# Windowed attention feeding a SwiGLU block on one core: a shorter lead and a new order of attention, with six instead of four chunks of q and k turned on the matmul array

## The chip, the cores and the metric

One core of one Trainium2 chip. The time is the device time of one execution in microseconds (us), fast executions only. A ratio is the mean time of one kernel's fast runs over that of the other's in the same rounds, so it is not quite the ratio of the medians quoted beside it. Two kernels are compared within one group of runs on the same chip, because the kernel before gave medians of 371.2 to 372.2 us from group to group. PE is the matmul engine, DVE the vector engine, ACT the scalar engine, POOL the general engine, SP the queue that issues all DMAs here, in order.

## The reference

Causal attention with a window of 64 keys, then a SwiGLU feed-forward block on its output:

```python
# q, k, v: (8 batches, 8 heads, 576 tokens, 64), float32
scores = q @ k^T / 8;  masked to 0 <= i - j < 64;  softmax;  times v
x = attention output as (4608 tokens, 512)
g = x @ w_gate                       # 512 x 1536
out = (g * sigmoid(g) * (x @ w_val)) @ w_out
```

## The kernel before

The 4608 tokens go through as 18 *chunks* of 256 (loads and turns of q and k), 36 *groups* of 128 (scores, products with v, turn of x, projection) and 9 *tiles* of 512 (twelve feed-forward steps each). Every engine executes its instructions in the order in which the program states them. So the text fixes how far attention runs ahead of the feed-forward (its *lead*).

q and k must be turned so that the head dimension lies on partitions. There are two ways. On the array, eight PE transposes go into PSUM and one copy brings them out:

```python
def turn2(n, nm, eng):                 # rows hold token pairs (load: 512 B runs)
    x_b = words.pop((nm, n))
    tp = ps_a.tile([P, 4, 2, P], BF16, name="tp", tag="a")
    for c in range(2):
        for p in range(4):
            nc.tensor.transpose(tp[:, p, c], x_b[:, c, P * p:P * p + P], identb[:])
    ...
    copy(eng, y, tp[:].rearrange("r p c x -> r p x c"))
```

By DMA, two transposes stand on the same queue as the loads:

```python
def turn1(n, nm):                      # rows hold single tokens (load1: 256 B runs)
    x_b = words.pop((nm, n))
    for i in range(2):
        ...
        sp.dma_start_transpose(out=ring[:, :, o:o + P], in_=x_b[:, i])
```

A feed-forward step uses two PSUM banks each for g and v. A step's banks are free again when DVE has done the `finish` of it, which is stated one step later:

```python
def step(t, m, c0=0, n=512):
    st = gv(t, m, c0, n)               # PE: 4 matmuls into g_ps, 4 into v_ps; ACT: tanh of g
    if pend: finish(pend)              # DVE: sg = (th + 1) * g;  hT = sg * v
    pend = st
```

`scores(g)` puts on PE the scores, on ACT their exponential E, on DVE the multiplication of E by the mask. `products(g)` is E times v on PE, with a normalisation on DVE into `x_b`. `turn_x(g)` is four transposes on PE and a copy on ACT into `xT`, the input of the feed-forward. All three share three PSUM banks (`ps_a`). F, A and B are full steps and half steps (first or second half of a tile). After a hand-ordered start the loop does one group per pass:

```python
for w in range(8, NG):
    t, s = divmod(w, 4); n, odd = w // 2, w % 2
    step(t, 3 * s)
    scores(w + 6);  turn_x(w + 4)
    ...                                 # casts of k (odd w) or q (even w) on POOL
    step(t, 3 * s + 1)
    products(w + 5, (0,));  cast_v(w + 6, pool)
    step(t, 3 * s + 2)
    products(w + 5, (1,))
    ...                                 # turn1 of k (odd, chunk n + 5) or q (even, chunk n + 4)
    project(t - 1, s)
    ...                                 # load1 and load_v of later chunks
```

(The bounds on w are cut.) Chunks 0 to 3 are turned on the array, 4 to 17 by DMA.

The softmax here doesn't subtract the row's maximum and nothing guards it: scores larger than these inputs give would overflow.

## Time and profile before

| | before |
|---|---|
| time, median of 2 | 371.24 us |
| span of the profiled execution | 370.2 us |
| PE busy | 93% |
| mean granted clock | 0.989 |
| PE idle before the scores of chunk 6 and of chunk 7 | 2.56 and 2.00 us |
| first loop step starts | 104.35 us |
| first pass of the loop | 12.66 us |
| later passes (21, from the projection in pass 8 to that in pass 29), each | 9.12 us |

A timeline row gives start, duration, engine, line, operation, output and inputs, and a count. A bracket gives the idle time of the engine before it and what ended it. A table by stages gives the stretch and its length, then busy time and number of instructions for PE, weight loads, DVE, ACT and POOL, then granted clock, DMA share and GB/s. The lines themselves stand in the prediction. First DVE, then PE, in pass 11 (w = 11 in the loop):

```profile
137.93 1.52 DVE L168 TENSOR_TENSOR E<-E,mask 128x512 bf16<-128x512 bf16 x2 [2.98 <-ACT E L167]
139.37 0.68 DVE L248 SCALAR_TENSOR_TENSOR sg<-th,g_ps 128x512 f32<-128x512 f32 x1
```
```profile
140.09 1.02 PE L237 MATMUL g_ps<-xT,wg 128*128 128x512 bf16 x3 [0.53 <-DVE sg L248]
```

DVE does the masks first and only then the `sg` that gives back a g bank. PE asks for that bank one step (1.73 us) after the scores, so it starts when `sg` ends, at 140.05. Slow masks: two of them took 1.52 us here, while POOL was casting v (137.14 to 139.17).

### The profile page before, as it was taken

How to read it: one execution, taken by the hardware profiler on the slowest of the kernel's cores; microseconds unless marked ns; L12 is line 12 of the kernel's file. 1: busy time of each engine (PE TensorE's matmuls, PEld its weight loads, DVE VectorE, ACT ScalarE, POOL GpSimd, SP SyncE). 2: the span in 40 equal slices, each digit the busy share in tenths (PEclk: the TensorE clock that was granted, in tenths of full speed). 3: DMA queues.
4: the chain of work that ended last, by engine and by line, in shares of the span. 5: the costliest groups of instructions: out<-in, count | busy, mean ns of one | idle time of the engine just before them, and what ended most of it. 6: DMA issues, size and time to landing. Idle time of an engine off the chain costs nothing.

```text
span 370.2 us, 7165 instructions
## 1 busy us (share of the span) xinstructions
PE 345.2 (93%) x2750; PEld 181.5 (49%) x2797; DVE 231.1 (62%) x503; ACT 154.0 (42%) x276; POOL 113.5 (31%) x159
## 2 busy tenths in 40 slices
PE   8787998989779999999999999999999999999995
PEld 3456556546334444444444545444444445444442
DVE  5577798697245666666666666666666666644520
ACT  3554755444243443444344444444444443323311
POOL 2554585463314350605060606060605120000000
PEclk9999999999899999999999999999999999999999
DMA  8999999899889965857688869675744300001112
GB/s 204 322 252 266 290 313 241 150 159 188 176 186 186 197 149 119 175 124 158 132 172 120 177 123 149 147 168 126 143 96 104 87 28 30 28 30 41 44 58 85
DMA packets 147841, 54.99 MB, mean 149 GB/s; under 512 B 127328, under 2 KB 141664, under 8 KB 147808
## 3 DMA queue, kind: packets, MB, share of 16 engines
q1 hardware_dynamic: 147808, 54.54, 66.6%
q8 instruction: 22, 0.36, 0.5%
q14 instruction: 11, 0.09, 0.1%
HBM read 37.75 MB, written 9.44 MB: 127 GB/s over the span
## 4 chain that ended last, share of the span: by engine, by line
PE 74%; DVE 6%; DMA 6%; SPq 5%; ACT 5%; issue 2%; POOL 2%; ACTq 0%; POOLq 0%
PE o_ps L254 24%; PE g_ps L237 21%; PE v_ps L237 19%; DMA q_f<-in_q_dram 4%; SPq L93 4%; DVE E L168 3%; PE s_ps L161 3%; PE w_ps L266 2%; ACT E L167 2%; PE xtp L205 2%; PE ao_ps L183 2%; PE ao_ps L187 2%; DMA qT<-q_fb 1%; DVE sg L248 1%; SPq L123 1%
## 5 line engine op out<-in xcount | busy, mean ns | idle before, releaser
L237 PE MATMUL g_ps<-xT,wg 128*128 128x512 bf16 (+1 forms) x457 | 111.9, 358 | 6.9 <-DVE sg L248 4.8
L237 PE MATMUL v_ps<-xT,wv 128*128 128x512 bf16 (+1 forms) x472 | 112.3, 360 | 0.9 <-ACT wv L103 0.5
L254 PE MATMUL o_ps<-wo,hT 128*128 128x512 bf16 x419 | 98.4, 384 | 0.7
L242 ACT ACTIVATE th<-g_ps 128x512 f32<-128x512 f32 (+1 forms) x120 | 67.3, 561 | 71.0 <-PE g_ps L237 66.9
L248 DVE SCALAR_TENSOR_TENSOR sg<-th,g_ps 128x512 f32<-128x512 f32 (+1 forms) x120 | 75.1, 626 | 20.9 <-ACT th L242 20.9
L168 DVE TENSOR_TENSOR E<-E,mask 128x512 bf16<-128x512 bf16 x72 | 36.9, 526 | 74.8 <-ACT E L167 73.4
L249 DVE TENSOR_TENSOR hT<-sg,v_ps 128x512 bf16<-128x512 f32 (+1 forms) x120 | 76.1, 634 | 8.4
L237 PEld LDWEIGHTS <-wv 128*128 128x128 bf16 x480 | 47.0, 98 | 48.3 <-issue 1.4
L237 PEld LDWEIGHTS <-wg 128*128 128x128 bf16 x480 | 44.8, 98 | 41.7 <-issue 7.0
L254 PEld LDWEIGHTS <-hT 128*128 128x128 bf16 x432 | 40.8, 99 | 46.1 <-issue 2.2
L105 POOL CAST q_fb<-q_f 128x1024 bf16<-128x1024 f32 x17 | 17.9, 1053 | 114.6 <-DMA q_f<-in_q_dram 112.4
L167 ACT ACTIVATE E<-s_ps 128x512 bf16<-128x512 f32 x72 | 39.1, 596 | 20.1 <-PE s_ps L161 20.1
L105 POOL CAST ve<-v_f 64x512 bf16<-64x512 f32 x71 | 44.3, 624 | 4.4
L192 DVE TENSOR_TENSOR x_b<-ao_ps,r 128x256 bf16<-128x256 f32 x72 | 30.5, 424 | 2.5
L105 POOL CAST vo<-v_f 128x512 bf16<-128x512 f32 x36 | 22.3, 621 | 25.8 <-DMA v_f<-in_v_dram 14.2
L105 POOL CAST k_fb<-k_f 128x1024 bf16<-128x1024 f32 x17 | 18.1, 1063 | 38.1 <-DMA k_f<-in_k_dram 32.6
L183 PE MATMUL ao_ps<-ve,E 128*128 128x65 bf16 x288 | 26.6, 194 | 2.2 <-DVE x_b L192 1.2
L183 PEld LDWEIGHTS <-E 128*128 128x128 bf16 x288 | 22.0, 98 | 9.6 <-DVE E L168 1.5
L187 PE MATMUL ao_ps<-vo,E 128*128 128x65 bf16 x288 | 26.6, 194 | 0.0
L206 ACT COPY xT<-xtp 128x512 bf16<-128x512 bf16 x36 | 21.2, 590 | 12.1 <-PE xtp L205 12.1
L187 PEld LDWEIGHTS <-E 128*128 128x128 bf16 x288 | 20.1, 98 | 6.5 <-issue 0.3
L161 PE MATMUL s_ps<-qT,kT 64*128 64x64 bf16 x576 | 14.9, 191 | 7.3 <-DMA qT<-q_fb 4.6
(73 smaller groups left out, 136.3 us busy)
## 6 DMA issues: line engine op xcount, KB each, us to landing
v_f<-in_v_dram SPq DMA_DIRECT2D x32, 256.0 KB, 4.8
k_f<-in_k_dram SPq DMA_DIRECT2D x25, 256.0 KB, 3.9
q_f<-in_q_dram SPq DMA_DIRECT2D x25, 256.0 KB, 4.2
w_f<-in_moe_w_gate_dram SPq DMA_DIRECT2D x6, 512.0 KB, 7.6
w_f<-in_moe_w_val_dram SPq DMA_DIRECT2D x6, 512.0 KB, 6.5
wo_f<-in_moe_w_out_dram SPq DMA_DIRECT2D x6, 512.0 KB, 6.5
k_f<-in_k_dram SPq DMA_DIRECT2D x3, 512.0 KB, 6.9
q_f<-in_q_dram SPq DMA_DIRECT2D x3, 512.0 KB, 8.1
```

The lines of the kernel that those rows point to most:

```text
L105: eng.tensor_copy(y, x)
L161: nc.tensor.matmul(ps[a][:, p, 1 - b], kT[g // 2 % KR][y, p, o:o + P], qT[g // 2 % QR][y, p, o:o + 64], tile_position=(64 * a, 0),)
L167: act.activation(e, ps[a][:], AF.Exp, scale=0.125)
L168: dve.tensor_mul(e, e, mk[:].unsqueeze(1).to_broadcast([P, 4, 2, 64]))
L183: nc.tensor.matmul(o_ps[:, i, :], E[:, e + P:e + 2 * P], ve[g % VR][:, y, :], start=True, stop=False,)
L187: nc.tensor.matmul(o_ps[:, i, :], E[:, e:e + P], vo[g % VR][:, y, :], start=False, stop=True,)
L192: dve.tensor_mul(x_b[:, 256 * h:256 * h + 256].rearrange("r (y d) -> r y d", y=4), o_ps[:, :, 0:D], r[:].unsqueeze(2).to_broadcast([P, 4, D]),
L237: nc.tensor.matmul(ps[:, 0:n], w[:, c, P * m:P * m + P], xT[t][:, c, c0:c0 + n], start=(c == 0), stop=(c == 3),)
L242: act.activation(th[:, 0:n], g_ps[:, 0:n], AF.Tanh, scale=0.5)
L248: dve.scalar_tensor_tensor(sg[:, 0:n], th[:, 0:n], 1.0, g_ps[:, 0:n], ALU.add, ALU.mult)
L249: dve.tensor_mul(hT[t][:, m, c0:c0 + n], sg[:, 0:n], v_ps[:, 0:n])
L254: nc.tensor.matmul(o_ps[:], hT[t][:, c, P * s:P * s + P], wo[:, c, :], start=(c == 0), stop=(c == 11),)
```

## The change

Intent: let attention run only four to five groups ahead instead of five to six, so that loads, casts and turns are wanted later; take chunks 4 and 5 off the DMA transposes; in the loop, do the products after the first step and the scores after the second.

```diff
+    load(4, k, "k_f")                  # was load1
+    load(4, q, "q_f")
...
-    turn1(4, "k_f")
-    turn1(4, "q_f")
     ...                                # and load(5, ...) follows at once
+    turn2(4, "k_f", dve)               # between F(1, 7) and F(1, 8)
+    turn2(4, "q_f", act)               # between F(1, 8) and F(1, 9)
...
+    turn2(5, "k_f", dve)               # before project(0, 1)
+    turn2(5, "q_f", act)               # between B(1, 3) and B(1, 4)
...
+    scores(12)
+    load1(8, k, "k_f")
     project(0, 3)
+    turn_x(11)

     for w in range(8, NG):
         step(t, 3 * s)
-        scores(w + 6);  turn_x(w + 4)
+        products(w + 4)
+        ...casts for chunks one earlier than before
         step(t, 3 * s + 1)
-        products(w + 5, (0,))
+        scores(w + 5);  turn_x(w + 4)
         step(t, 3 * s + 2)
-        products(w + 5, (1,))
         ...                            # turns and loads for chunks one earlier
         project(t - 1, s)
```

(Cut to its core; bounds left out. The order of the second tile's steps is shuffled too: the first half runs to A(1, 6), the second to B(1, 6), every projection of tile 0 stands between attention parts, and the casts move with them.)

More of the change, by code (lines that the diff above doesn't have):

```diff
@@ L413 @@
     turn_x(5)
-    load1(4, k, "k_f")
-    load1(4, q, "q_f")
+    load(4, k, "k_f")
+    load(4, q, "q_f")
     load_v(4)
+    cast_k(3, "k_f", pool)
     F(0, 10)
-    cast_k(3, "k_f", pool)
     cast_k(3, "q_f", pool)
+    keys_before(3)
+    turn2(3, "k_f", dve)
+    F(0, 11)
+    turn2(3, "q_f", act)
     cast_v(6, pool)
     cast_v(7, pool)
-    F(0, 11)
-    keys_before(3)
-    turn2(3, "k_f", dve)
     A(1, 0)
-    turn2(3, "q_f", act)
+    for s in range(2):
+        casts_o(s, pool)
     A(1, 1)
-    for s in range(3):
-        casts_o(s, pool)
-    A(1, 2)
-    scores(6)
-    A(1, 3)
-    scores(7)
-    products(6)
-    for s in range(3, 6):
-        casts_o(s, pool)
-    A(1, 4)
-    turn_x(6)
-    products(7)
+    scores(6)
+    A(1, 2)
+    scores(7)
+    A(1, 3)
+    products(6)
+    A(1, 4)
+    products(7)
+    turn_x(6)
+    for s in range(2, 4):
+        casts_o(s, pool)
     A(1, 5)
@@ L443 @@
     cast_k(4, "q_f", pool)
-    turn1(4, "k_f")
-    turn1(4, "q_f")
-    keys_before(4)
-    load1(5, k, "k_f")
-    load1(5, q, "q_f")
-    load_v(5)
-    B(1, 0)
-    F(1, 6)
+    load(5, k, "k_f")
+    load(5, q, "q_f")
+    load_v(5)
+    A(1, 6)
+    B(1, 0)
+    for s in range(4, 6):
+        casts_o(s, pool)
+    B(1, 1)
+    F(1, 7)
+    keys_before(4)
+    turn2(4, "k_f", dve)
     cast_v(8, pool)
     cast_v(9, pool)
-    F(1, 7)
+    F(1, 8)
+    turn2(4, "q_f", act)
+    F(1, 9)
     scores(8)
-    F(1, 8)
+    project(0, 0)
+    B(1, 2)
+    scores(9)
     products(8)
-    F(1, 9)
-    turn_x(8)
-    scores(9)
     cast_k(5, "k_f", pool)
     cast_k(5, "q_f", pool)
-    turn1(5, "k_f")
-    turn1(5, "q_f")
-    keys_before(5)
     load1(6, k, "k_f")
@@ L469 @@
     F(1, 10)
+    turn_x(8)
     products(9)
@@ L474 @@
     turn_x(9)
-    scores(10)
-    project(0, 0)
-    B(1, 1)
-    products(10)
-    B(1, 2)
+    keys_before(5)
+    turn2(5, "k_f", dve)
+    project(0, 1)
+    B(1, 3)
+    turn2(5, "q_f", act)
     cast_k(6, "k_f", pool)
+    turn1(6, "k_f")
+    keys_before(6)
     cast_k(6, "q_f", pool)
-    turn1(6, "k_f")
     turn1(6, "q_f")
-    keys_before(6)
     load1(7, k, "k_f")
@@ L487 @@
     load_v(7)
+    B(1, 4)
+    scores(10)
+    project(0, 2)
+    products(10)
+    B(1, 5)
+    scores(11)
     turn_x(10)
-    scores(11)
-    project(0, 1)
-    B(1, 3)
+    B(1, 6)
     products(11)
     cast_v(12, pool)
-    B(1, 4)
-    turn_x(11)
-    scores(12)
-    project(0, 2)
-    B(1, 5)
-    products(12)
-    cast_v(13, pool)
     cast_k(7, "k_f", pool)
@@ L503 @@
     keys_before(7)
-    cast_k(7, "q_f", pool)
-    turn1(7, "q_f")
+    scores(12)
     load1(8, k, "k_f")
-    load1(8, q, "q_f")
-    scores(13)
     project(0, 3)
-    cast_k(8, "k_f", pool)
-    turn1(8, "k_f")
-    keys_before(8)
-    load1(9, k, "k_f")
+    turn_x(11)
     for w in range(8, NG):
@@ L519 @@
         step(t, 3 * s)
-        if w + 6 < NG:
-            scores(w + 6)
+        if w + 4 < NG:
+            products(w + 4)
+        if odd and n + 4 < NB:
+            cast_k(n + 4, "k_f", pool)
+        if not odd and n + 3 < NB:
+            cast_k(n + 3, "q_f", pool)
+        if w + 5 < NG:
+            cast_v(w + 5, pool)
+        step(t, 3 * s + 1)
+        if w + 5 < NG:
+            scores(w + 5)
         if w + 4 < NG:
             turn_x(w + 4)
-        if odd and n + 5 < NB:
-            cast_k(n + 5, "k_f", pool)
-        if not odd and n + 4 < NB:
-            cast_k(n + 4, "q_f", pool)
-        step(t, 3 * s + 1)
-        if w + 5 < NG:
-            products(w + 5, (0,))
-        if w + 6 < NG:
-            cast_v(w + 6, pool)
-        step(t, 3 * s + 2)
-        if w + 5 < NG:
-            products(w + 5, (1,))
-        if odd and n + 5 < NB:
-            turn1(n + 5, "k_f")
-            keys_before(n + 5)
-        if not odd and n + 4 < NB:
-            turn1(n + 4, "q_f")
+        step(t, 3 * s + 2)
+        if odd and n + 4 < NB:
+            turn1(n + 4, "k_f")
+            keys_before(n + 4)
+        if not odd and n + 3 < NB:
+            turn1(n + 3, "q_f")
         project(t - 1, s)
         if odd and n + 5 < NB:
-            load1(n + 5, q, "q_f")
+            load1(n + 5, k, "k_f")
         if odd and n + 4 < NB:
             load_v(n + 4)
-        if not odd and n + 6 < NB:
-            load1(n + 6, k, "k_f")
+        if not odd and n + 4 < NB:
+            load1(n + 4, q, "q_f")
     flush()
```

## The prediction

> **What bounds the kernel now.** I read the page first, then the chain of waits, the timeline of the matmul engine (PE) around its largest gaps, the table by stages, and the DMA queue's own timeline. The kernel has one core, so there is no slow die to set aside.
>
> ```profile
> PE 345.2 (93%) x2750; PEld 181.5 (49%) x2797; DVE 231.1 (62%) x503; ACT 154.0 (42%) x276; POOL 113.5 (31%) x159
> PEclk9999999999899999999999999999999999999999
> ```
>
> PE is the bound. Its one dip in granted clock is the eleventh of the forty slices, 93 to 102 us. The table by stages (columns: stretch, length, busy time and instructions of PE, weight loads, DVE, ACT, POOL, then clock, DMA share, GB/s) says the same:
>
> ```profile
> 51.50:68.00 16.50, 14.05 (x159) 9.91 (x160) 13.97 (x35) 8.08 (x16) 12.31 (x15) 1.00 0.97 248
> 68.00:91.70 23.70, 22.38 (x236) 13.38 (x237) 18.80 (x42) 11.05 (x22) 9.27 (x12) 1.00 0.99 176
> 91.70:104.35 12.65, 9.57 (x83) 4.92 (x83) 5.31 (x14) 3.67 (x8) 5.32 (x8) 0.87 0.88 193
> 104.35:117.00 12.65, 10.60 (x72) 5.00 (x72) 6.88 (x15) 3.95 (x7) 2.93 (x4) 0.87 0.87 166
> 117.00:306.00 189.00, 185.11 (x1474) 93.37 (x1501) 121.89 (x257) 80.99 (x147) 57.43 (x82) 1.00 0.67 135
> ```
>
> From 117 us on PE has little left to give. The loss is in the two stretches from 91.7 to 117 us. PE's timeline names the event in each:
>
> ```profile
> 91.59 0.62 PE L205 MATMUL xtp<-identb,x_b 128*128 128x128 bf16 x4
> 94.77 0.41 PE L161 MATMUL s_ps<-qT,kT 64*128 64x64 bf16 x16 [2.56 <-DMA qT<-q_fb]
> 95.11 4.45 PE L254 MATMUL o_ps<-wo,hT 128*128 128x512 bf16 x11
> ...
> 101.75 2.76 PE L254 MATMUL o_ps<-wo,hT 128*128 128x512 bf16 x11
> ...
> 108.24 0.41 PE L161 MATMUL s_ps<-qT,kT 64*128 64x64 bf16 x16 [2.00 <-DMA qT<-q_fb]
> ...
> 110.12 1.91 PE L237 MATMUL v_ps<-xT,wv 128*128 128x512 bf16 x4
> ```
>
> The scores of chunk 6, then of chunk 7, wait for q to come back from a DMA transpose. After each wait the same matmuls run slowly: 4.45 instead of 2.76 us, and 1.91 instead of the 1.03 seen elsewhere. The chain shows that this is the end of a long series, not two late transfers:
>
> ```profile
> 57.87 5.67 DMA q_f<-in_q_dram
> 63.64 1.04 POOL q_fb L105
> 66.62 2.09 SPq L123
> 70.73 5.00 DMA q_f<-in_q_dram
> 75.88 1.24 POOL q_fb L105
> 79.23 1.44 SPq L123
> ...
> 85.00 4.92 DMA q_f<-in_q_dram
> 90.07 1.04 POOL q_fb L105
> 92.18 2.46 DMA qT<-q_fb
> ```
>
> Load, cast, transpose (L123, on the same in-order queue as the loads), next load: about 13 us per chunk of 256 tokens. A transpose on the queue holds the next loads back until its own cast is done.
>
> **What the Trainium skill says.** (1) "TensorE: Matmul & The Clock Gate", section "What's actually happening": PE falls to half clock after an idle window of about 3.4 us and needs as much busy time to return. The trace agrees in kind: the granted clock was 0.60 from 95.1 to 99.4 and 0.57 from 108.8 to 112.0 us, though the gaps were only about 2.8 and 2.3 us. (2) The same page, "Part 4: PE-mode transpose": a 128x128 transpose of about 275 ns in one kernel, whose result lies in PSUM and must be copied out. Here one takes 219 ns, eight in a row hold PE 0.45 us, and the copies take 1.22 us (DVE, k) and 1.01 us (ACT, q). (3) "SBUF — State Buffer", "Who interferes with whom": a DVE instruction with two SBUF inputs and a GpSimd instruction that reads SBUF exclude each other. The mask multiply (L168) has two such inputs; its shortest was 409 ns and its longest 1250 ns, which agrees. (4) "DMA: Bandwidth & Descriptors", "Why small descriptors are slow (HBM only)": a 256 B descriptor pays a fixed cost per packet. No row of this trace isolates that; I give it no number.
>
> **The change part by part.** Engine order is program order here, so I step the three busy engines by hand with durations from the trace: a full feed-forward step 1.73 us of PE (8 matmuls of 0.216) and 1.38 of DVE (half steps 0.87 and 0.85), scores 0.34, products 0.48 (DVE 1.10), a turn of x 0.33, a projection 2.59.
>
> *Removed:* the DMA transposes of chunks 4 and 5, 8 of 56. On the queue they took 2.72 + 3.36 and 2.87 + 3.10 us, 12.0 in all. Chunk 5's loads now follow chunk 4's at once and no longer wait behind casts, and both use 512 B runs.
>
> *Added:* 32 transposes on PE, 4 x 0.45 = 1.8 us, on the path; two DVE copies (2.4 us) and two ACT copies (2.0 us), which only partly fit beside PE.
>
> *51.5 to 68 us.* DVE is busy 85% here. Stepping it: half steps of group 1 arrive at 0.87, DVE retires them at 0.85 but must also do two score masks and two products (about 4 us), so DVE sets the pace before and after. The extra half step after the turn of x hides one ACT copy. I get the step F(1,7) starting at 67.5 instead of 68.0: gain 0.5.
>
> *67.5 us to the start of the loop.* PE work: five full steps 8.65, five halves 4.35, five scores 1.7, four products 1.9, four turns of x 1.3, four projections 10.4, four chunk turns 1.8: 30.1 us. I find stalls at the second bank of products(8) (0.35), the q copy before scores(10) (0.4), the mask before products(11) (0.5), the free bank in scores(12) (0.6), and small ones: about 2.1. Loop start 99.7 instead of 104.35.
>
> *Does chunk 6 still make PE wait?* Its loads follow the output of project(0,0) at about 77.7, are issued by 85, and the last q lands near 85 to 86 (5 to 6 us after issue, as before). The queue then reaches the transposes after the output of project(0,1), at 87.7, two pairs of 2.7 us: q is turned by about 93. PE asks at about 95.9: 2.8 us to spare. Chunk 7: turned near 106, asked for at 112.6.
>
> *The loop.* Work of one pass is 3 x 1.73 + 0.34 + 0.48 + 0.33 + 2.59 = 8.93 us. From the project at 114.58 to the one at 306.03, 21 passes take 9.12 each: 3.3 us over the shortest (8.96). DVE's masks sit between the first step and the finish that frees its bank, so a mask slowed by a POOL cast stalls PE (0.53 us at 140.1). After the change the products come after the first step and the masks only after the second, followed by a step and a projection (4.3 us) before that bank is asked for. Collisions stop hurting; I credit 2.5 us.
>
> *Sum.* Start of the loop: 104.35 - 99.7 = 4.65 earlier, less one scores and one products (0.82) not yet done: 3.8. First pass: before it took 104.35 to 117.01 = 12.66, of which 3.7 over a normal 8.96: saved. Later passes 2.5. Total 10.0. I take off 0.8 for waits that a hand stepping misses: 9.2. The timed 371.24 becomes 362.0 us (2.5% less).
>
> **The rivals.** *A: the waits only move.* With a lead of four to five groups instead of five to six, the transposes reach scores later. Steady state: q's transposes run in an even pass after 0.7 + 1.2 + 3 us of loads, landing 8.4 us into it; scores want them 4.0 us into the next, 4.5 us to spare. Landings ranged up to 5.0 us in the trace against the 2.5 median, so mostly safe. If chunk 6 is late all the same, 1 to 2 us of wait and as much of slow clock return: 364 to 366. If the loop waits in each second pass by 0.5 us, 7 us go: 369. *B: DVE becomes the bound before 100 us.* It is 85 and 79% busy in the two stretches ahead of 91.7 us and gets 2.4 us more. If neither copy hides, the loop starts at 102: about 364. *C: only the waits were lost, and the loop was at its floor.* Then 2.5 us of credit fall away: 364.5. *D: more comes.* No stall at all before the loop and the floor in every pass: 359.
>
> **Range and chances.** 362.0 us, 8 in 10 within 358.5 to 367.0. The limit for faster by 2% is 363.8; B or C in full would miss it narrowly, in part they would not. Faster 0.68, within 2% 0.30, slower 0.02: slower needs waits in most passes, against 4.5 us of slack.
>
> **What would show it.** Right: no granted clock below 0.95 between 90 and 120 us; no PE wait on a qT transfer; the loop's first step near 99 to 100 us; 48 DMA transposes, chunk turns on PE up by 32; project-to-project time near 8.97 with longer masks but no PE wait on the feed-forward gate multiply after 110 us. Wrong: scores waiting on DMA in the loop (A), PE waiting on DVE between 55 and 95 us by more than 4 us (B), passes still at 9.1 (C).

## The result

362.06 us (two runs, 361.73 and 362.39) against 371.24: ratio 0.9753, 95% interval 0.9711 to 0.9795. Two later groups, of six runs of the changed kernel and eleven of the kernel before each, gave 361.74 against 371.28 (0.9752) and 361.52 against 372.06 (0.9717).

| | before | after |
|---|---|---|
| time, median | 371.24 us | 362.06 us |
| profiled span | 370.2 us | 359.8 us |
| F(1,7) starts | 68.00 us | 67.20 us |
| first loop step starts | 104.35 us | 100.71 us |
| first pass | 12.66 us | 8.92 us |
| later passes, each | 9.12 us | 8.92 us |
| PE idle before the scores of chunk 6 / 7 for q | 2.56 / 2.00 us | none / none |
| mean granted clock | 0.989 | 0.998 |

The page of the profile after, busy times and the clock row:

```profile
PE 340.8 (95%) x2790; PEld 181.2 (50%) x2837; DVE 233.1 (65%) x507; ACT 155.9 (43%) x279; POOL 112.9 (31%) x159
PEclk9999999999999999999999999999999999999999
```

The dip in the clock row is gone. The table by stages, cut at the same events as in the prediction (turn of chunk 3 to F(1,7), to the loop, first pass, passes to the projection in pass 29):

```profile
51.50:67.20 15.70, 14.47 (x170) 10.74 (x169) 13.82 (x35) 8.11 (x18) 8.40 (x10) 1.00 1.13 262
67.20:100.70 33.50, 30.56 (x316) 18.55 (x320) 23.46 (x55) 16.50 (x31) 14.64 (x21) 1.00 0.79 146
100.70:109.63 8.93, 8.86 (x71) 4.42 (x72) 5.82 (x12) 3.26 (x6) 4.94 (x7) 1.00 1.25 213
109.63:294.60 184.97, 182.82 (x1474) 92.03 (x1501) 124.45 (x259) 80.95 (x147) 58.23 (x83) 1.00 0.74 142
```

The start of the loop is 3.64 us earlier (0.80 of it already at F(1,7)). The first pass is 3.74 us shorter. The 21 passes that follow took 191.45 us from projection to projection before (114.42 to 305.87) and take 187.39 now (107.04 to 294.43): 4.06 us. The remainder is 1.04 us longer, of which one scores and one products (0.82 us), moved into the loop's end, explain most. 3.64 + 3.74 + 4.06 - 1.04 = 10.4 us, the difference of the two spans. The timed medians differ by only 9.2: the profiled execution of the kernel before was itself 0.9 us slower than its median.

The queue of the changed kernel, where chunk 6 is turned, and PE where it is asked for, up to the first loop step; the last line is PE where chunk 7 is asked for:

```profile
87.33 2.61 SPq L123 DMA_TRANSPOSE kT<-k_fb  x2
90.03 2.53 SPq L123 DMA_TRANSPOSE qT<-q_fb  x2
```
```profile
95.58 0.20 PE L161 MATMUL s_ps<-qT,kT 64*128 64x64 bf16 x1
96.45 0.40 PE L161 MATMUL s_ps<-qT,kT 64*128 64x64 bf16 x15 [0.68 <-DVE x_b L192]
97.02 2.54 PE L254 MATMUL o_ps<-wo,hT 128*128 128x512 bf16 x11 [0.16 <-issue]
...
100.71 1.02 PE L237 MATMUL g_ps<-xT,wg 128*128 128x512 bf16 x4 [0.94 <-ACT xT L206]
...
113.67 0.41 PE L161 MATMUL s_ps<-qT,kT 64*128 64x64 bf16 x16
```

The first of the two q transposes of chunk 6, which holds the tokens that these scores use, has landed at 92.4 (2.4 us after its issue), three us before PE asks. q of chunk 7 is through the queue at 107.6. What PE waits for now is local: a bank of `ps_a` (0.68), and the copy of the turn of x(11), which stands directly ahead of the step that needs it (0.94).

### The profile page after: what moved, and what is told of

Same layout as the page of the kernel before. It is cut to its first block, busy times and chain, and to the rows that moved or that the text cites. A ratio compares the mean times of both kernels' runs of the same rounds, so it can differ in the third digit from the quotient of the medians.

```text
span 359.8 us, 7265 instructions
## 1 busy us (share of the span) xinstructions
PE 340.8 (95%) x2790; PEld 181.2 (50%) x2837; DVE 233.1 (65%) x507; ACT 155.9 (43%) x279; POOL 112.9 (31%) x159
## 4 chain that ended last, share of the span: by engine, by line
PE 66%; DVE 3%; DMA 1%; issue 1%; ACT 0%; SPq 0%; ACTq 0%
PE o_ps L254 23%; PE v_ps L237 18%; PE g_ps L237 17%; PE s_ps L161 2%; PE xtp L205 2%; DVE x_b L192 2%; PE ao_ps L187 1%; PE ao_ps L183 1%; DVE sg L248 1%; DMA k_f<-in_k_dram 1%; DVE r L191 1%; ACT os__3828 L259 0%; ACT os__5098 L259 0%; SPq L261 0%; ACTq L259 0%
## 5 line engine op out<-in xcount | busy, mean ns | idle before, releaser
L237 PE MATMUL g_ps<-xT,wg 128*128 128x512 bf16 (+1 forms) x454 | 109.9, 354 | 5.0 <-DVE sg L248 2.8
L254 PEld LDWEIGHTS <-hT 128*128 128x128 bf16 x432 | 42.0, 98 | 50.2
L237 PEld LDWEIGHTS <-wg 128*128 128x128 bf16 x484 | 43.7, 98 | 37.6 <-issue 4.8
L168 DVE TENSOR_TENSOR E<-E,mask 128x512 bf16<-128x512 bf16 x72 | 34.2, 483 | 21.2 <-ACT E L167 19.2
L191 DVE RECIPROCAL r<-ao_ps 128x4 f32<-128x4 f32 x72 | 12.7, 176 | 53.7 <-PE ao_ps L187 53.7
L206 ACT COPY xT<-xtp 128x512 bf16<-128x512 bf16 x36 | 21.3, 591 | 10.4 <-PE xtp L205 10.4
L183 PE MATMUL ao_ps<-ve,E 128*128 128x65 bf16 x288 | 23.2, 193 | 2.1 <-DVE x_b L192 1.2
L183 PEld LDWEIGHTS <-E 128*128 128x128 bf16 x288 | 20.1, 97 | 6.3 <-DVE x_b L192 1.5
L187 PE MATMUL ao_ps<-vo,E 128*128 128x65 bf16 x288 | 23.2, 193 | 0.0
L187 PEld LDWEIGHTS <-E 128*128 128x128 bf16 x288 | 19.0, 97 | 3.9 <-issue 0.4
```

Source lines behind the costliest of these rows:

```text
L168: dve.tensor_mul(e, e, mk[:].unsqueeze(1).to_broadcast([P, 4, 2, 64]))
L183: nc.tensor.matmul(o_ps[:, i, :], E[:, e + P:e + 2 * P], ve[g % VR][:, y, :], start=True, stop=False,)
L187: nc.tensor.matmul(o_ps[:, i, :], E[:, e:e + P], vo[g % VR][:, y, :], start=False, stop=True,)
L206: act.copy(xT[t][:, :, off:off + P], tp[:])
L237: nc.tensor.matmul(ps[:, 0:n], w[:, c, P * m:P * m + P], xT[t][:, c, c0:c0 + n], start=(c == 0), stop=(c == 3),)
L254: nc.tensor.matmul(o_ps[:], hT[t][:, c, P * s:P * s + P], wo[:, c, :], start=(c == 0), stop=(c == 11),)
```

## The experiments

Three parts of the change could each claim the gain: fewer transposes on the queue (*queue*), asking later (*lead*), and the order within a pass (*order*). All twelve runs gave a correct result. The shorter lead was never run by itself: experiment 4 has it with the old order in the loop, but with the rearranged start and the array turns. So its share alone stays open.

**1. Array turns alone, in the kernel before.**

```diff
-    load1(4, ...)   turn1(4, ...)   load1(5, ...)   turn1(5, ...)
+    load(4, ...)    turn2(4, ...)   load(5, ...)    turn2(5, ...)     # same places
```

> The kernel before with one thing changed: q and k of chunks 4 and 5 are loaded as token pairs and turned on PE at the place where the DMA transposes were issued; order of steps, lead and loop as before. Queue theory (the waits come from transposes that hold the loads back on the queue): chunk 6 is turned by about 92.5 us, asked for about 93.5, no wait; chunk 7 asked for near 103, turned near 104.5, a wait of 1.5 us at most. Gain of about 7.4 (two waits with their slow clock) less 1.8 (PE turns) less 1.5: 366 to 368 us. Lead theory (scores ask too early, whatever the queue does): both waits stay near 2 us or more, 1.8 us of PE is added, 371 to 373 us. Passes of the loop stay near 9.1 us in both.

Measured: 370.13 against 372.22 us, ratio 0.9936 (0.9903 to 0.9969). One of its six executions, the profiled one, took 1248.58 us; PE was busy for all of it, with 512-column matmuls 0.80 us apart instead of 0.216. It is in no ratio. That profile shows nothing of the normal course, so the kernel ran again.

> The same kernel as the first experiment (the kernel before with chunks 4 and 5 turned on PE), because that one's profile fell on an execution of 1247 us and cannot be read. Timed it stood at 370.1 against 372.2. Queue theory in full would show no q wait at chunk 6; I now expect the wait for chunk 6 gone, one of 1 to 2.5 us for chunk 7 with slow clock after it, passes of 9.1 us, and a gain of 2 to 3 us.

Measured: 369.22 against 372.06 us, ratio 0.9922 (0.9886 to 0.9959). PE at chunk 6 and at chunk 7, and the queue where q of chunk 6 is turned:

```profile
95.54 0.41 PE L161 MATMUL s_ps<-qT,kT 64*128 64x64 bf16 x16
95.88 2.76 PE L254 MATMUL o_ps<-wo,hT 128*128 128x512 bf16 x12
...
107.01 0.41 PE L161 MATMUL s_ps<-qT,kT 64*128 64x64 bf16 x16 [1.69 <-DVE hT L249]
```
```profile
91.05 2.53 SPq L123 DMA_TRANSPOSE qT<-q_fb  x2
```

The wait for chunk 6 is gone, but not by the queue alone: q landed at 93.6, 1.1 us earlier than before (94.6), and PE came 3.4 us later. With q at 93.6 PE would still have had to wait at its old time, 92.2, though its delay also held back the output (87.86) behind which these transposes stand on the queue.

The wait for chunk 7 stays (1.69 us; the bracket names DVE, but DVE's last piece ended at 106.86 and the q transposes, issued 104.42, left the queue at 106.95, so the trace does not separate the two), without slow clock this time.

The gain is small, against the 3 to 5 us that the queue theory expected at first: the projection (0,0) starts at 84.44 instead of 81.04. Not all of these 3.4 us come from the array turns. 1.29 us are lost ahead of the first turn, at 65.87: the half step A(1, 5) starts at 64.47 instead of 63.18, after a wait of 1.45 us for `x_b`, because two pairs of masks took 1.37 and 1.59 us (0.92 and 0.75 before). The kernel of experiment 5, which is the kernel before up to there, was 0.89 us late at the same place. That leaves about 2.1 us for everything behind it, the turns included, near the 1.8 us of their matmuls. In that part PE waited 0.53 us for an `sg` that stood behind a copy of k on DVE. Passes stayed at 9.14 us.

**2. The shorter lead and the new order without the array turns.**

```diff
-    load(4), load(5), turn2(4), turn2(5)
+    load1(4), load1(5), turn1(4) ahead of load1(5), turn1(5) and load1(6) ahead of project(0, 0)
```

> The changed kernel with q and k of chunks 4 and 5 loaded in 256 B runs and turned by DMA as before, everything else (order of steps, shorter lead, loop) as changed. PE does 1.8 us less. Queue theory: chunk 6 is turned near 94.6 to 95.5 as in the kernel before, asked for near 93.5: a wait of 1 to 2 us with some slow clock after it, 362 to 365 us. Lead theory: asking later is what cures it, no wait over 0.5 us, and 360 to 361.5 us, faster than the changed kernel. Passes of the loop at 8.92 us in both.

Measured: 362.94 against 372.22 us, ratio 0.9744 (0.9704 to 0.9783), runs from 360.10 to 364.71. Repeated beside the changed kernel:

> The changed kernel with chunks 4 and 5 turned by DMA, a second time, now beside the changed kernel on one chip. Its first profile had one q wait of 2.3 us at chunk 6 and 1.3 us of slow clock, against 1.8 us of PE work saved. By those numbers and the smaller E and bank waits it should be 0.5 to 1.5 us slower than the changed kernel, with runs spread over 3 us or more where the changed kernel's stay within 1.

Measured: 362.61 us (360.69 to 364.55, ratio 0.9745) against 361.52 for the changed kernel in the same group:

> The changed kernel, as the reference of this call: 361.5 to 362.5 us, six runs within 1 us.

(Its six runs lay between 361.34 and 361.79, ratio 0.9717.) So nearly the whole gain comes without a single extra array turn. With the array turns of chunks 4 and 5 the median is 1.1 us lower, which is not clear of noise (the intervals overlap), and the spread of the runs is 0.5 us instead of 3.9. PE at chunk 6 in the two profiles of this experiment, first run and repeat:

```profile
96.48 0.61 PE L161 MATMUL s_ps<-qT,kT 64*128 64x64 bf16 x16 [2.33 <-DMA qT<-q_fb]
97.03 4.01 PE L254 MATMUL o_ps<-wo,hT 128*128 128x512 bf16 x12
```
```profile
96.10 0.41 PE L161 MATMUL s_ps<-qT,kT 64*128 64x64 bf16 x16 [2.14 <-DMA qT<-q_fb]
96.44 2.76 PE L254 MATMUL o_ps<-wo,hT 128*128 128x512 bf16 x12
```

Chunk 6 still waits, by a little more than the 1 to 2 us that the queue theory expected; the lead theory's forecast of no wait failed. Its q landed at about 96.3 and 95.9. In the changed kernel it landed at 92.4, before the time at which PE was ready here (94.15 and 93.96), so given this lead the array turns cure chunk 6. Chunk 7 does not wait, though its q is no earlier than before (out of the queue at 108.9 in the repeat, 108.2 before), as PE asks for it only at 113.3, not at 106.2: the later asking cures it.

The two profiles also show the same kernel with nearly the same gap, once with a projection 1.25 us slower after it (span 361.2) and once without (359.3). So the gap sometimes brings slow clock and sometimes not. The mean clocks for all twelve runs agree: the five at 0.991 or less took 362.92 to 364.71 us, the other seven 360.10 to 363.24.

**3. Masks behind the finish, in the kernel before.**

```diff
     step(t, 3 * s)
-    scores(w + 6)
+    scores(w + 6, False)               # PE and ACT parts only
     ...
     step(t, 3 * s + 1)
+    mask_late()                        # the two DVE multiplies by the mask
```

> The kernel before with only the DVE mask multiplies of the loop moved behind the finish of the first step of a pass; PE and ACT order unchanged, DMA unchanged. If masks ahead of the finish are what stretches the passes: 21 passes from 9.12 towards 8.95, PE waits on the sg multiply in the loop gone, the two q waits unchanged, 371.2 becomes 367.5 to 368.5. If the passes are stretched by something else (DMA, POOL, PE issue): within 0.7 us of 371.2.

Measured: 368.41 against 372.22 us, ratio 0.9899 (0.9866 to 0.9932). Two projections of its profile, 21 passes apart:

```profile
113.19 2.75 PE L263 MATMUL o_ps<-wo,hT 128*128 128x512 bf16 x12
...
300.57 2.75 PE L263 MATMUL o_ps<-wo,hT 128*128 128x512 bf16 x12
```

The passes went from 9.12 to 8.92 us, without a PE wait listed in them, though some masks were as slow as before (1.62 us for two in pass 11). The waits for q at chunk 6 and 7 stayed (2.91 and 1.14 us). Both as expected: DVE order alone is worth the 4 us that the changed kernel gains in its passes.

**4. The old order within a pass, in the changed kernel.**

```diff
     step(t, 3 * s)
-    products(w + 4)
+    scores(w + 5)
     step(t, 3 * s + 1)
-    scores(w + 5);  turn_x(w + 4)
+    products(w + 4)
     step(t, 3 * s + 2)
+    turn_x(w + 4)
```

> The changed kernel with the loop's attention parts in the order of the kernel before: scores and masks after the first step, products after the second, turn of x after the third; lead and DMA order unchanged. If masks ahead of a finish that is wanted a step later cost the passes their 0.2 us: passes from 8.92 to about 9.05 to 9.15, 3 to 4 us slower than the changed kernel. If it was the collision of masks with POOL casts and the changed DMA times have removed it: a pass stays within 0.05 of 8.92 and masks stay near 0.43 us each, under 1 us slower.

Measured: 365.15 against 361.74 us for the changed kernel in the same group (ratios to the kernel before 0.9839 and 0.9752). Passes take 9.06 us, as expected, but masks are at their short length (424 to 426 ns between 117 and 297 us), so slow masks are not needed for the loss. One pass, DVE and then PE:

```profile
141.08 0.68 DVE L248 SCALAR_TENSOR_TENSOR sg<-th,g_ps 128x512 f32<-128x512 f32 x1
```
```profile
141.81 1.02 PE L237 MATMUL g_ps<-xT,wg 128*128 128x512 bf16 x4
```

PE starts the third step at 141.81, right after `sg` ends at 141.76, and 0.11 us after its last product: about 0.08 us per pass, too short for a bracket. The turn of x standing alone takes 0.29 instead of 0.24 us until the next matmul starts. Together that is nearly the 0.14 us by which these passes are longer. The split into the two is read from one pass, not tested by itself.

**5. The waits filled with dummy matmuls, in the kernel before.**

```diff
+    warm(11)                            # matmuls nobody reads, before scores(12)
     scores(12)
     ...
+    if w == 8: warm(8)                  # before scores(14)
```

> The kernel before with 11 and 8 dummy matmuls (2.4 and 1.7 us of PE work whose result nobody reads) put into the two waits for q of chunks 6 and 7. If the slow stretches of 3 to 4 us after each wait come from PE having been idle: the granted clock stays above 0.95 from 90 to 120 us, the projection takes 2.6 to 2.8 us instead of 4.45, and the kernel gets 2.5 to 3.5 us faster, 368 to 369, though it does more work. If the slow stretches have another cause (contention with the DMA that lands then): same time or slower, 371 to 372.

Measured: 371.13 against 372.22 us, ratio 0.9974 (0.9945 to 1.0003): unclear, and less than expected. The profiled execution, the fastest of six (369.70), shows the clock at 1.0 throughout:

```profile
92.53 2.54 PE L266 MATMUL w_ps<-wz 128*128 128x512 bf16 x11
95.00 0.41 PE L161 MATMUL s_ps<-qT,kT 64*128 64x64 bf16 x16
95.34 2.76 PE L254 MATMUL o_ps<-wo,hT 128*128 128x512 bf16 x12
```

That agrees with idleness as the cause of the slow clock, but experiment 2 had an unfilled wait without one, so a single clean profile shows little. The mean clocks for the other runs say more: four of the six filled runs stand at 1.0 (the others at 0.995 and 0.989), against none above 0.995 in the eleven runs of the kernel before. So filling the waits does remove most of the slow clock. Five of those eleven runs stand at 0.994 or 0.995, so the kernel before does not always pay in full; why only about 1 us came of it stays open.

**6. 256 B runs for chunks 4 and 5, in the changed kernel.**

```diff
-    load(4, ...), load(5, ...)          # token pairs
+    load1(4, ...), load1(5, ...)        # single tokens; turn2 writes them out accordingly
```

> The changed kernel with chunks 4 and 5 loaded in 256 B runs instead of 512 B, still turned on PE. My theory: chunks 4 and 5 land well before they are used, so nothing changes: within 0.7 us of the changed kernel in the same rounds. Rival (the longer runs are what frees the DMA engines in time): 1 us or more slower, with PE or POOL waiting for k_f or q_f between 60 and 90 us.

Measured: 361.44 us against 361.74 in the same group. The longer runs have no part in the gain. The Trainium skill, "DMA: Bandwidth & Descriptors", "Why small descriptors are slow (HBM only)", gives a 256 B descriptor a fixed cost per packet. That is not contradicted: the cast of k of chunk 4 could begin at 61.46 us with short runs and at 61.60 with long ones, so nothing was held up by it here.

> The changed kernel once more, as the reference for the three others of this call: 361.5 to 362.5 us, profile as before within 0.5 us.

(The changed kernel in that group: 361.48 to 362.24 us, median 361.74, span 360.3.)

**7. The turn of x(11) ahead of the projection, in the changed kernel.**

```diff
+    turn_x(11)
     project(0, 3)
-    turn_x(11)
```

> The changed kernel with the turn of x(11) ahead of the projection (0,3) instead of behind it. The changed profile shows PE idle for 0.94 us at 100.7 for the ACT copy of this turn. Theory: the copy hides under the projection, 0.9 us less, 361.1 if the changed kernel is at 362.0. Rival: the turn now waits for x_b of products(11) instead, gain under 0.3 us.

Measured: 360.98 us against 361.74. The lines that answer to the 0.94 us of the changed kernel:

```profile
97.18 0.40 PE L205 MATMUL xtp<-identb,x_b 128*128 128x128 bf16 x4
97.42 2.75 PE L254 MATMUL o_ps<-wo,hT 128*128 128x512 bf16 x12
100.01 1.03 PE L237 MATMUL g_ps<-xT,wg 128*128 128x512 bf16 x4
```

The copy hides under the projection; 0.76 of the 0.9 us are saved.

**8. A version from these findings.** Chunk 4 goes back to DMA, chunk 5 stays on the array, and the parts ahead of the loop are ordered so that each wait lies under other work:

```diff
-    load(4), turn2(4)
+    load1(4), turn1(4) ahead of load(5)
...
     turn_x(10)
-    B(1, 6)
+    project(0, 3)
     products(11)
     ...
+    B(1, 6)
+    turn_x(11)
     scores(12)
     load1(8, k, "k_f")
-    project(0, 3)
-    turn_x(11)
```

> A version meant to beat both: the changed kernel with chunk 4 turned by DMA again (0.9 us of PE less; its q is needed at 73 and would be turned by about 69), chunk 5 still on PE so that chunk 6's queue is free, and ahead of the loop project(0,3) moved before products(11), the half step B(1,6) behind products(11), and turn_x(11) before scores(12). If the chunk that matters for the wait is 5 and not 4: no q wait at chunk 6, the bank wait (0.68) and the mask wait before products(11) (0.45) gone, the wait for xT at the first loop step 0.5 instead of 0.94: 359.5 to 360.5 us against 361.8. If chunk 4 mattered too: a q wait over 1 us at chunk 6, 362 or more.

Measured: 358.96 us (358.60 to 359.66) against 361.52 for the changed kernel in the same group; ratio to the kernel before 0.9649 (0.9624 to 0.9675). It is the fastest of all, and a little better than expected.

```profile
97.77 0.62 PE L205 MATMUL xtp<-identb,x_b 128*128 128x128 bf16 x4
98.32 0.41 PE L161 MATMUL s_ps<-qT,kT 64*128 64x64 bf16 x16
99.06 1.02 PE L237 MATMUL g_ps<-xT,wg 128*128 128x512 bf16 x4 [0.33 <-ACT xT L206]
```

No wait for q at chunk 6, which leaves the queue at 92.8 as in the changed kernel (92.6): of the two chunks moved to the array, only chunk 5 is needed for that. The loop starts at 99.06. This run bundles two edits, so how much each gives is not separated.

## Why the prediction was right, point by point

The time (362.0) and the range held. Its steps fared like this.

- *Start to F(1,7):* predicted 67.5, measured 67.20. DVE was busy for 13.82 of the 15.70 us after 51.5, as the prediction had it.
- *Start of the loop:* predicted 99.7, measured 100.71. The stepping found the mask wait, the bank wait (0.6, measured 0.68) and the q copy before scores(10) (0.4, measured 0.23 in brackets), but missed the wait for xT at the first step (0.94), which experiment 7 confirms.
- *Chunk 6 and 7 in time:* predicted turned by about 93 and near 106; the queue was done with q at 92.6 and 107.6. Shown. The prediction credits the removed transposes for it and treats the shorter lead as a risk (rival A). The experiments correct that: chunk 7 is cured by asking later, chunk 6, given the shorter lead, by the array turns, and without the array turns the ratio is 0.9745 against 0.9717 in the same group, 9.5 of 10.5 us.
- *First pass:* saved 3.7, measured 3.74.
- *The later passes:* credited 2.5, measured 4.06: the term most in error. The prediction took 8.96 for the shortest pass before and put the rest down to masks slowed by POOL casts. Counted from the first matmul of a pass to that of the next, no pass before was under 9.01 us. Fifteen of the 21 took 9.01 to 9.03 with masks of normal length, six took 9.13 to 9.69 with slow ones (1.03 to 1.59 us for two). So slow masks cost 2.2 us, near the credit. The 1.9 us that it missed come from masks of normal length ahead of a finish that is wanted a step later; each pass went to 8.92, the sum of its matmuls. Experiments 3 and 4 show the mechanism. The detail that masks would get longer was wrong: their mean fell from 526 to 483 ns.
- *The allowance of 0.8 us* and the missed 0.94 us against the undersized passes: the errors nearly cancel. The hit on 362.0 to a tenth is partly luck.
- *Rival B* (DVE the bound before 100 us) did not happen in the changed kernel. Experiment 1 does not show it either: of its 3.4 us there, 1.29 are lost ahead of the turns. *Rival C* (the loop at its floor before) is refuted by experiment 3, rival A by the changed profile.
- *The clock:* the gaps of "about 2.8 and 2.3 us" are the lengths of the windows it queried; PE's own idle time was 2.56 and 2.00 us.

## What to carry to other kernels

Where an in-order engine frees a buffer, put its other work behind that instruction if the buffer is wanted soon and the other result later: moving two DVE instructions per pass behind a finish gave 1% here without any change on the matmul engine. A late operand can be cured by making it earlier or by asking for it later; look at the second first, as here it cost no work. And before moving transposes onto the matmul array, look at which engine must copy them out and how busy it is just there: a copy of k took DVE 1.22 us, and in experiment 1 PE waited 0.53 us behind one. Finally, before charging a delay to an edit, look at whether it begins ahead of the edited place.

## What the Trainium skill lacked or had wrong

- "TensorE: Matmul & The Clock Gate", "What's actually happening": it gives an idle window of about 3.4 us before the clock drops. Here shorter gaps were enough: bracketed waits of 2.00 and 2.56 us (the kernel before), 2.33 (experiment 2) and 2.91 (experiment 3) were followed by slow matmuls, while one of 2.14 us (experiment 2, repeat) was not, nor were those of 1.69 and 1.14 (experiments 1 and 3). In these traces a gap of 2 us or more was one that may cost more than its length.
- The same page, "Seeing it yourself", warns that clock events in a trace can be unreliable and reports a PE stuck at a quarter of its clock for over 50 us. It does not say that this can last for a whole execution, as here: in one execution of experiment 1, matmuls ran 0.80 instead of 0.216 us apart for all of 1247 us, while the recorded mean granted clock stood at 1.0.
